# A decode block on one core: ScalarE takes more of the last heads' sums, the second modulation is issued earlier, and the gate's products go to TensorE

## The chip, the cores and the metric

The kernel runs on one core of one Trainium2 chip. The metric is the device time of one execution in microseconds (us); the median of three runs of the kernel before is 1065.96 us (1065.53 to 1066.04). Each core has TensorE (PE, matmuls; PEld is its weight loads), VectorE (DVE), ScalarE (ACT), GpSimd (POOL), the queue of SyncE (SP) that issues the DMAs here, and 16 DMA engines.

## The reference

One token (D = 640) passes through an adaptive-LayerNorm block. The attention reads a cache of 32 heads, 8192 positions, 192 elements, keys and values, all float32:

```
mod = silu(c) @ w_mod                      # six vectors: sa, ca, ga, sb, cb, gb
h = layernorm(x) * (1 + ca) + sa
q = (h @ wq)  per head
p = softmax(q . K^T * 192 ** -0.5);  o = p . V
x = x + ga * (o @ wo)
h = layernorm(x) * (1 + cb) + sb
x = x + gb * (relu(h @ w1 + b1) ** 2 @ w2 + b2)
```

## The kernel before

The caches are 403 MB of the 452 MB that are read, so most of the program is a stream of heads. SyncE's queue issues, head by head, one load of a head's keys (6 MB, with a query or output weight behind them in most heads) and one of its values (6 MB). All of them, and the four weight tiles at the start and the end, share a ring of three slots (`slot`, line 54): each load waits until the tile three places earlier has been read to the end. At the end of the ring the second modulation `wm1_t` (L315 to L321; it also holds the last output weight) takes the slot of head 30's values, `w1_t` (L322; with the gate's weight behind it, L325) that of head 31's keys, and `w2_t` (L328) that of head 31's values. Each is loaded in pieces, and a reader waits for the piece that it needs.

The program order is the order on each engine; nothing is rescheduled. Partition p holds 64 positions of a head. `keys(h)` (L201) multiplies them by the query on VectorE (L213, in place) and then sums the 192 products of each position in three ways: GpSimd folds the upper half of `nf` positions onto the lower (L214) and VectorE reduces the folded 96 (L221); ScalarE sums `na` positions, one ACTIVATE with an accumulator each (L217); VectorE reduces the remaining `a` positions directly (L218). On VectorE the order is L213, L218, whatever `between` puts there (L219: in odd heads the gather of the output weight, three instructions at L154), then L221, which waits for GpSimd. Heads 0 to 29 do this in one part with 28 folded, 4 on ScalarE and 32 direct. Head 30 does it in two halves, head 31 in four quarters, because their keys are loaded in as many pieces (`K_PARTS`):

```
K_PARTS = {H - 2: 2, H - 1: 4}
N_ACT = {H - 2: 8, H - 1: 16}
```

`softmax(h)` (L224) takes the maximum over all partitions through TensorE and writes the exponentials by ScalarE (L236). `own(h-1)` (L257) is VectorE's work on the previous head's output: a masked multiply (L272) and two reductions (L275). `turn` (L278) makes columns of two heads' output by three matmuls (L282) and a ScalarE copy (L284). `values(h)` (L242) is 24 matmuls on TensorE (L249, L253).

After the last head the order is: `own(31)`, `turn`, the attention output `att` (L337, L340), its copy by ScalarE (L343), the second modulation `ps_mod` (20 matmuls, L348), x1 = x + ga * att (L351, L352), its LayerNorm (from L128), the first MLP layer `ps_f` (20 matmuls, L361), relu squared and transposition on VectorE (L364, L365, L106), then on VectorE the gate's products with silu(c) (`weigh`, L147 and L149), and on TensorE the first half of the second layer `ps_y` (24 matmuls, L376), the gate's column sums `ps_g` (4 matmuls, L383), the second half of `ps_y`, and the two last VectorE steps (L391, L392) and the store.

The profile has two records for each float32 matmul, so that 20 matmuls are listed as x40.

Of the kernel before, what the change touches and what calls it, by code (L numbers as in the profile page):

```python
# [45 lines left out]
def block_kernel(ctx: ExitStack, tc: tile.TileContext, first, kx, vx, wm1, w1, w2, out):  # L46
# [56 lines left out]
    def columns(src, n, name, pool=const, **how):  # L103

        t = pool.tile([P, n // 32, 32], F32, name=name, **how)
        nc.vector.transpose(t.rearrange("p b r -> p (b r)"), src)  # L106
        return t
# [37 lines left out]
    def weigh(to, w):  # L145

        nc.vector.tensor_scalar(to, w[:, 0], e[:, 0:1], None, op0=ALU.mult)  # L147
        for b in range(1, KB):
            nc.vector.scalar_tensor_tensor(to, w[:, b], e[:, b:b + 1], to, op0=ALU.mult, op1=ALU.add)  # L149
# [51 lines left out]
    def keys(h, between):  # L201

        q = qb_t[h // 2][:, DH * (h % 2):DH * (h % 2 + 1)]
        sc = work.tile([P, NPOS], F32, tag="sc", name=f"sc{h}")
        t = k_t[h][:, :KV].rearrange("p (i d) -> p i d", d=DH)
        parts = K_PARTS.get(h, 1)
        n = NPOS // parts
        nf, na = N_FOLD // parts, N_ACT.get(h, 4) // parts
        a, b = n - nf - na, n - na
        for c in range(parts):  # L210
            pr = t[:, c * n:(c + 1) * n]
            s = sc[:, c * n:(c + 1) * n]
            nc.vector.tensor_mul(pr, pr, q[:, None, :].to_broadcast([P, n, DH]))  # L213
            nc.gpsimd.tensor_add(pr[:, a:b, :DH // 2], pr[:, a:b, :DH // 2], pr[:, a:b, DH // 2:])  # L214
            for i in range(b, n):
                jk = work.tile([P, DH], F32, tag="jk", name=f"jk{h}_{c}_{i}", bufs=2)
                nc.scalar.activation(jk, pr[:, i], AF.Copy, accum_out=s[:, i:i + 1])  # L217
            nc.vector.tensor_reduce(s[:, :a], pr[:, :a], axis=AX.X, op=ALU.add)  # L218
            if c == 0:  # L219
                between()  # L220
            nc.vector.tensor_reduce(s[:, a:b], pr[:, a:b, :DH // 2], axis=AX.X, op=ALU.add)  # L221
        return sc
# [34 lines left out]
    def own(h):  # L257

        i, a = h // 2, h % 2
        if not a:  # L260
            os_t[i] = work.tile([P, PW], F32, tag="os", name=f"os{i}")
        to = os_t[i][:, DH * a:DH * (a + 1)]
        if a:
            ri_t[i] = work.tile([P, 2], F32, tag="ri", name=f"ri{i}")
            nc.vector.reciprocal(ri_t[i], sum_t.pop(i))
            nc.vector.tensor_scalar(os_t[i][:, :DH], os_t[i][:, :DH], ri_t[i][:, 0:1], None, op0=ALU.mult)
        scale = ri_t.pop(i)[:, 1:2] if a else 1.0
        m = big(f"own{h}", 1024)
        o = o_t.pop(h)
        d = [(0, 512, to[:, :DA]), (512, 1024, to[:, DA:])]  # L270
        for lo, hi in ([(0, 512), (512, 1024)] if h == H - 1 else [(0, 1024)]):
            nc.vector.scalar_tensor_tensor(m[:, lo:hi], o[:, lo:hi], scale, mask[:, lo:hi], op0=ALU.mult, op1=ALU.mult)  # L272
            for x0, x1, r in d:
                if lo <= x0 < hi:
                    nc.vector.tensor_reduce(r, m[:, x0:x1].rearrange("p (j d) -> p d j", d=r.shape[1]),  # L275
                                            axis=AX.X, op=ALU.add)
# [53 lines left out]
        nc.sync.dma_start(w2_t[:, b0 * D:(b0 + n) * D], w2[:, b0 * D:(b0 + n) * D])  # L330
# [11 lines left out]
    att_s = const.tile([P, DG], F32, name="att_s")  # L342
    nc.scalar.copy(att_s, att[:, :DG])  # L343

    ps_mod = psum.tile([P, 512], F32, tag="q", name="ps_mod", bufs=2)
    for b in range(KB):
        for g in range(G):
            nc.tensor.matmul(ps_mod[32 * g:32 * (g + 1), :3 * DG], e[:, b:b + 1].to_broadcast([P, 32]),  # L348
                             wm1_t[:, b, :, DG * g:DG * (g + 1)], start=(b == 0), stop=(b == KB - 1))
    x1 = const.tile([P, DG], F32, name="x1")  # L350
    nc.vector.tensor_mul(x1, ps_mod[:, :DG], att_s)  # L351
    nc.vector.tensor_add(x1, x1, x_t)  # L352
# [18 lines left out]
    py = psum.tile([P, 512], F32, tag="q", name="ps_y", bufs=2)  # L371

    def second(b0, b1):
        for b in range(b0, b1):
            for g in range(G):
                nc.tensor.matmul(py[32 * g:32 * (g + 1), :DG], fT[:, b], w2_t[:, b, DG * g:DG * (g + 1)],  # L376
                                 start=(b == 0), stop=(b == FB - 1))

    n = W2_CUT[0][1]
# [11 lines left out]
    nc.vector.tensor_mul(y, py[:, :DG], gb)  # L391
    nc.vector.tensor_add(y, y, x1)  # L392
# [44 lines left out]
```

## Time and profile before

| | |
|---|---|
| runs before, median of 3 | 1065.96 us |
| profiled execution, its time | 1065.27 us |
| its span, first to last instruction | 1063.5 us |
| read from memory | 451.82 MB, 425 GB/s over the span |
| busy share: DVE, PE, POOL, ACT | 85%, 34%, 18%, 9% |
| DMA queue of SyncE, share of the 16 engines' time | 98.5% |

The span is what the rows of the trace cover; the execution's own time is 1.77 us longer. Times in the rows are microseconds from the start of the span. A row of the timeline gives start, duration, engine, line, operation, the tile written and those read, the count where equal instructions are merged, and in brackets how long the engine was idle before and on whom it waited. A row of the windows gives for one stretch of time each engine's busy time with its count of instructions, then TensorE's granted clock as a share of full speed, the busy share of the DMA engines and GB/s.

### The profile page before, as it was taken

How to read it: one execution, taken by the hardware profiler on the slowest of the kernel's cores; microseconds unless marked ns; L12 is line 12 of the kernel's file. 1: busy time of each engine (PE TensorE's matmuls, PEld its weight loads, DVE VectorE, ACT ScalarE, POOL GpSimd, SP SyncE). 2: the span in 40 equal slices, each digit the busy share in tenths (PEclk: the TensorE clock that was granted, in tenths of full speed). 3: DMA queues.
4: the chain of work that ended last, by engine and by line, in shares of the span. 5: the costliest groups of instructions: out<-in, count | busy, mean ns of one | idle time of the engine just before them, and what ended most of it. 6: DMA issues, size and time to landing. Idle time of an engine off the chain costs nothing.

```text
span 1063.5 us, 5476 instructions
## 1 busy us (share of the span) xinstructions
PE 366.9 (34%) x2088; PEld 133.7 (13%) x2088; DVE 907.2 (85%) x400; ACT 95.2 (9%) x394; POOL 189.9 (18%) x43
## 2 busy tenths in 40 slices
PE   0324333143432314343222434313343431333355
PEld 0101111011110101111010111101111110110122
DVE  6897898998989899898898988899898889989963
ACT  1010001000010101001010100101010010000210
POOL 0220122221022222012222102222211222221210
PEclk9767656666665666666566666656666665666668
DMA  9999999999999999999999999999999999999994
GB/s 400 439 429 419 443 424 440 430 436 442 427 431 434 437 434 431 430 436 428 442 429 436 435 434 430 436 431 437 434 432 434 428 434 438 434 422 416 432 400 201
DMA packets 11410, 452.17 MB, mean 425 GB/s; under 512 B 1268, under 2 KB 1272, under 8 KB 1656
## 3 DMA queue, kind: packets, MB, share of 16 engines
q1 hardware_dynamic: 11384, 451.83, 98.5%
q8 instruction: 16, 0.26, 0.1%
q14 instruction: 10, 0.08, 0.0%
HBM read 451.82 MB, written 0.00 MB: 425 GB/s over the span
## 4 chain that ended last, share of the span: by engine, by line
DVE 40%; DMA 40%; PE 14%; issue 2%; ACT 1%; POOL 1%; POOLq 0%; DVEq 0%; ACTq 0%; SPq 0%
DMA k<-in_kx 39%; DVE k L213 20%; DVE sc L218 9%; PE ps_o L249 8%; DVE sc L221 4%; DVE acc L154 3%; PE ps_o L253 2%; DMA first_t<-in_first 1%; ACT p L236 1%; POOL k L214 1%; PE ps_sum L121 1%; PE ps_mx L228 1%; DVE ma_w L149 1%; PE ps_f L361 1%; PE ps_q L191 1%
## 5 line engine op out<-in xcount | busy, mean ns | idle before, releaser
L213 DVE TENSOR_TENSOR k<-k,qb 128x12288 f32<-128x12288 f32 (+2 forms) x36 | 415.2, 11534 | 94.1 <-DMA k<-in_kx 90.0
L214 POOL TENSOR_TENSOR k<-k 128x2688 f32<-128x2688 f32 (+2 forms) x36 | 188.6, 5240 | 826.9 <-DVE k L213 782.0
L228 PE MATMUL ps_mx<-ident,mp 128*128 128x128 f32 x32 | 15.1, 473 | 589.3 <-DVE mp L226 589.3
L218 DVE TENSOR_REDUCE sc<-k 128x32 f32<-128x6144 f32 (+2 forms) x36 | 207.1, 5753 | 1.2
L249 PE MATMUL ps_o<-v,p 128*32 128x512 f32 x1024 | 183.5, 882 | 2.6 <-ACT p L236 2.6
L217 ACT ACTIVATE jk<-k 128x192 f32<-128x192 f32 x144 | 50.4, 351 | 532.5 <-DVE k L213 508.9
L221 DVE TENSOR_REDUCE sc<-k 128x28 f32<-128x2688 f32 (+2 forms) x36 | 94.9, 2635 | 2.9 <-POOL k L214 2.9
L228 PEld LDWEIGHTS ps_mx<-ident,mp 128*128 128x128 f32 x32 | 5.8, 181 | 613.9 <-DVE mp L226 593.1
L275 DVE TENSOR_REDUCE os<-own 128x128 f32<-128x512 f32 x64 | 63.7, 1036 | 1.1
L253 PE MATMUL ps_o<-v,p 128*32 128x512 f32 x512 | 60.4, 592 | 0.0
L249 PEld LDWEIGHTS ps_o<-v,p 128*32 128x32 f32 x1024 | 40.0, 154 | 116.3 <-issue 112.9
L191 PE MATMUL ps_q<-k,hR 128*128 128x384 f32 x150 | 52.3, 496 | 1.5 <-DMA k<-in_kx 1.5
L236 ACT ACTIVATE p<-sc,nm 128x512 f32<-128x512 f32 x32 | 23.1, 721 | 304.8 <-DVE nm L230 176.8
L282 PE MATMUL ps_oT<-ones,os 128*128 128x1 f32 x96 | 27.6, 356 | 45.5 <-DVE os L275 33.3
L154 DVE SCALAR_TENSOR_TENSOR acc<-k,oT,acc 128x640 f32<-128x640 f32 x45 | 39.7, 882 | 1.1
L191 PEld LDWEIGHTS ps_q<-k,hR 128*128 128x128 f32 x150 | 27.3, 190 | 29.5 <-issue 10.9
L282 PEld LDWEIGHTS ps_oT<-ones,os 128*128 128x128 f32 x96 | 23.5, 304 | 53.5 <-DVE os L275 36.0
L217 ACT ACTIVATION_READ_ACCUMULATOR jk<-k 128x1 f32 x144 | 26.8, 186 | 0.0
L230 DVE TENSOR_REDUCE nm<-ps_mx 128x1 f32<-128x128 f32 x32 | 9.3, 292 | 18.2 <-PE ps_mx L228 18.2
L272 DVE SCALAR_TENSOR_TENSOR own<-ps_o,ri,mask 128x1024 f32<-128x1024 f32 (+1 forms) x17 | 20.7, 1215 | 3.0 <-PE ps_o L253 3.0
L253 PEld LDWEIGHTS ps_o<-v,p 128*32 128x32 f32 x512 | 15.3, 110 | 41.1 <-issue 41.1
L272 DVE SCALAR_TENSOR_TENSOR own<-ps_o,mask 128x1024 f32<-128x1024 f32 x16 | 19.4, 1215 | 0.0
(87 smaller groups left out, 129.9 us busy)
## 6 DMA issues: line engine op xcount, KB each, us to landing
k<-in_kx SPq DMA_DIRECT2D x29, 7104.0 KB, 27.4
v<-in_vx SPq DMA_DIRECT2D x31, 6144.0 KB, 23.1
k<-in_kx SPq DMA_DIRECT2D x1, 6144.0 KB, 25.5
k<-in_kx SPq DMA_DIRECT2D x2, 3072.0 KB, 20.3
k<-in_kx SPq DMA_DIRECT2D x3, 1536.0 KB, 16.4
first_t<-in_first SPq DMA_DIRECT2D x1, 4173.5 KB, 12.8
v<-in_vx SPq DMA_DIRECT2D x1, 4096.0 KB, 19.8
wm_t<-in_wm SPq DMA_DIRECT2D x1, 3840.0 KB, 21.4
```

The source lines that it names most:

```text
L154: nc.vector.scalar_tensor_tensor(to, w[:, j], s[:, j:j + 1], to, op0=ALU.mult, op1=ALU.add)
L191: nc.tensor.matmul(ps[:, :PW], hR[:, b], w[:, b], start=(b == 0), stop=(b == KB - 1))
L213: nc.vector.tensor_mul(pr, pr, q[:, None, :].to_broadcast([P, n, DH]))
L214: nc.gpsimd.tensor_add(pr[:, a:b, :DH // 2], pr[:, a:b, :DH // 2], pr[:, a:b, DH // 2:])
L217: nc.scalar.activation(jk, pr[:, i], AF.Copy, accum_out=s[:, i:i + 1])
L218: nc.vector.tensor_reduce(s[:, :a], pr[:, :a], axis=AX.X, op=ALU.add)
L221: nc.vector.tensor_reduce(s[:, a:b], pr[:, a:b, :DH // 2], axis=AX.X, op=ALU.add)
L249: nc.tensor.matmul(o_t[h][32 * g:32 * (g + 1), :512], p[:, 4 * c:4 * c + 4].rearrange("p e r -> p (e r)"), t[:, 512 * c:512 * (c + 1)], st ...
L253: nc.tensor.matmul(o_t[h][32 * g:32 * (g + 1), 512:], p[:, 8 * c:8 * c + 8, ::2].rearrange("p e r -> p (e r)"), t[:, 512 * (na + c):512 * ...
L272: nc.vector.scalar_tensor_tensor(m[:, lo:hi], o[:, lo:hi], scale, mask[:, lo:hi], op0=ALU.mult, op1=ALU.mult)
L275: nc.vector.tensor_reduce(r, m[:, x0:x1].rearrange("p (j d) -> p d j", d=r.shape[1]), axis=AX.X, op=ALU.add)
L282: nc.tensor.matmul(pt[:, j:j + 1], os_[:, P * j:P * (j + 1)], ones[:, :1], start=True, stop=True)
```

## The change

In the last three heads the parts and their split are given by one table; a pair is (folded, ScalarE), and the rest of a part's positions is direct. Head 29 is computed in two halves now, though its keys are still one load. ScalarE has 16 positions of head 29 (4 before), 20 of head 30 (8) and 26 of head 31 (16). The folded positions are still 28 in heads 29 and 30, and 16 in head 31 (28 before).

After the last head, `ps_mod` is written ahead of `own(31)` and `turn`; the sum of x1 for the LayerNorm is accumulated by the instruction that adds x; `weigh` for the gate is gone, and in its place TensorE does 20 matmuls with silu(c) as the stationary operand right behind `ps_f`, ahead of all of `ps_y`.

```diff
-N_FOLD = 28
-N_ACT = {H - 2: 8, H - 1: 16}
+SUMS = {H - 3: ((14, 10), (14, 6)), H - 2: ((14, 12), (14, 8)), H - 1: ((4, 7), (4, 7), (4, 7), (4, 5))}
...
-    def layernorm(x, copies, scale1, shift, name):
+    def layernorm(x, copies, scale1, shift, name, s=None):
...
-        s = const.tile([P, 1], F32, name=name + "_s")
-        nc.vector.tensor_reduce(s, x, axis=AX.X, op=ALU.add)
+        if s is None:
+            s = const.tile([P, 1], F32, name=name + "_s")
+            nc.vector.tensor_reduce(s, x, axis=AX.X, op=ALU.add)
...
-        parts = K_PARTS.get(h, 1)
-        n = NPOS // parts
-        nf, na = N_FOLD // parts, N_ACT.get(h, 4) // parts
-        a, b = n - nf - na, n - na
-        for c in range(parts):
+        sums = SUMS.get(h, ((28, 4),))
+        n = NPOS // len(sums)
+        for c, (nf, na) in enumerate(sums):
+            a, b = n - nf - na, n - na
...
+    ps_mod = psum.tile([P, 512], F32, tag="q", name="ps_mod", bufs=2)
+    for b in range(KB):
+        for g in range(G):
+            nc.tensor.matmul(ps_mod[32 * g:32 * (g + 1), :3 * DG], e[:, b:b + 1].to_broadcast([P, 32]),
+                             wm1_t[:, b, :, DG * g:DG * (g + 1)], start=(b == 0), stop=(b == KB - 1))
     own(H - 1)
     oT = turn(NPAIR - 1)
...
-    ps_mod = psum.tile([P, 512], F32, tag="q", name="ps_mod", bufs=2)
...
     nc.vector.tensor_mul(x1, ps_mod[:, :DG], att_s)
-    nc.vector.tensor_add(x1, x1, x_t)
+    s1 = const.tile([P, 1], F32, name="s1")
+    nc.vector.scalar_tensor_tensor(x1, x1, 1.0, x_t, op0=ALU.mult, op1=ALU.add, accum_out=s1)
...
-    gb_w = big("gb_w", D)
-    weigh(gb_w, wg_t)
...
-    second(0, n)
     ps_g = psum.tile([P, 512], F32, tag="sm", name="ps_g", bufs=2)
-    for g in range(G):
-        nc.tensor.matmul(ps_g[32 * g:32 * (g + 1), :DG], ones[:, :32], gb_w[:, DG * g:DG * (g + 1)], start=True, stop=True)
+    for b in range(KB):
+        for g in range(G):
+            nc.tensor.matmul(ps_g[32 * g:32 * (g + 1), :DG], e[:, b:b + 1].to_broadcast([P, 32]),
+                             wg_t[:, b, DG * g:DG * (g + 1)], start=(b == 0), stop=(b == KB - 1))
...
-    second(n, FB)
+    for b in range(FB):
+        for g in range(G):
+            nc.tensor.matmul(py[32 * g:32 * (g + 1), :DG], fT[:, b], w2_t[:, b, DG * g:DG * (g + 1)],
+                             start=(b == 0), stop=(b == FB - 1))
```

The line numbers of the changed kernel differ by one or a few from those of before. On VectorE, head 29 reads as follows before; k_2054 are its keys, sc its sums, acc the output weight's accumulator, and 128x32 means 32 positions.

```order
L213 TENSOR_TENSOR k_2054<-k_2054,qb_1872 128x12288
L218 TENSOR_REDUCE sc_2058<-k_2054 128x32
L154 SCALAR_TENSOR_TENSOR acc<-k_2054,oT_2027,acc 128x640 x3
L221 TENSOR_REDUCE sc_2058<-k_2054 128x28
L226 TENSOR_REDUCE mp_2074<-sc_2058 128x1
```

After, on VectorE at the same place:

```order
L212 TENSOR_TENSOR k_2054<-k_2054,qb_1872 128x6144
L217 TENSOR_REDUCE sc_2058<-k_2054 128x8
L154 SCALAR_TENSOR_TENSOR acc<-k_2054,oT_2027,acc 128x640 x3
L220 TENSOR_REDUCE sc_2058<-k_2054 128x14
L212 TENSOR_TENSOR k_2054<-k_2054,qb_1872 128x6144
L217 TENSOR_REDUCE sc_2058<-k_2054 128x12
L220 TENSOR_REDUCE sc_2058<-k_2054 128x14
L225 TENSOR_REDUCE mp_2102<-sc_2058 128x1
```

The multiply is cut in two, 12 direct positions are gone, and the gather stands in the first half only. On TensorE, from the last matmuls of head 31's values on, the program before reads as follows; ps_oT is `turn`, and counts are matmuls.

```order
L253 MATMUL ps_o_2266<-v_2196,p_2254 32x512 x8
L282 MATMUL ps_oT_2311<-ones,os_2258 128x1 x3
L337 MATMUL att<-acc,ones 32x160 x4
L340 MATMUL att<-wm_t,oT_2315 32x160 x12
L348 MATMUL ps_mod<-wm_t,silu 32x480 x20
L121 MATMUL ps_ln_tm<-ln_s,ones 128x1
L121 MATMUL ps_ln_tv<-ln_ss,ones 128x1
L361 MATMUL ps_f<-w_t,hT_2382 32x384 x20
L376 MATMUL ps_y<-w_t,fT 32x160 x24
L383 MATMUL ps_g<-gb_w,ones 32x160 x4
L376 MATMUL ps_y<-w_t,fT 32x160 x24
```

After, on TensorE at the same place:

```order
L252 MATMUL ps_o_2338<-v_2248,p_2326 32x512 x8
L335 MATMUL ps_mod<-wm_t,silu 32x480 x20
L281 MATMUL ps_oT_2404<-ones,os_2330 128x1 x3
L341 MATMUL att<-acc,ones 32x160 x4
L344 MATMUL att<-wm_t,oT_2408 32x160 x12
L120 MATMUL ps_ln_tm<-s_2431,ones 128x1
L120 MATMUL ps_ln_tv<-ln_ss,ones 128x1
L361 MATMUL ps_f<-w_t,hT_2453 32x384 x20
L371 MATMUL ps_g<-w_t,silu 32x160 x20
L383 MATMUL ps_y<-w_t,fT 32x160 x48
```

`ps_mod` has moved from behind `att` to ahead of `turn`, and `ps_g`, 20 matmuls instead of 4, from the middle of `ps_y` to ahead of it. No DMA is added, removed or put in another place on SyncE's queue.

More of the change, by code (lines that the diff above doesn't have):

```diff
@@ L343, in block_kernel @@
     nc.scalar.copy(att_s, att[:, :DG])
-    ps_mod = psum.tile([P, 512], F32, tag="q", name="ps_mod", bufs=2)
-    for b in range(KB):
-        for g in range(G):
-            nc.tensor.matmul(ps_mod[32 * g:32 * (g + 1), :3 * DG], e[:, b:b + 1].to_broadcast([P, 32]),
-                             wm1_t[:, b, :, DG * g:DG * (g + 1)], start=(b == 0), stop=(b == KB - 1))
     x1 = const.tile([P, DG], F32, name="x1")
     nc.vector.tensor_mul(x1, ps_mod[:, :DG], att_s)
-    nc.vector.tensor_add(x1, x1, x_t)
+    s1 = const.tile([P, 1], F32, name="s1")
+    nc.vector.scalar_tensor_tensor(x1, x1, 1.0, x_t, op0=ALU.mult, op1=ALU.add, accum_out=s1)
     cb1 = const.tile([P, DG], F32, name="cb1")
     nc.scalar.activation(cb1, ps_mod[:, 2 * DG:3 * DG], AF.Copy, bias=1.0)
-    hT2 = columns(layernorm(x1, 32, lambda: cb1, lambda: ps_mod[:, DG:2 * DG], "ln2"), DG, "hT2")
+    hT2 = columns(layernorm(x1, 32, lambda: cb1, lambda: ps_mod[:, DG:2 * DG], "ln2", s1), DG, "hT2")
     pf = psum.tile([P, 512], F32, tag="q", name="ps_f", bufs=2)
@@ L366, in block_kernel @@
     fT = columns(f, FG, "fT", work, tag="qb")
-    gb_w = big("gb_w", D)
-    weigh(gb_w, wg_t)
[L371 to L379, printed above, removed]
-    second(0, n)
     ps_g = psum.tile([P, 512], F32, tag="sm", name="ps_g", bufs=2)
-    for g in range(G):
-        nc.tensor.matmul(ps_g[32 * g:32 * (g + 1), :DG], ones[:, :32], gb_w[:, DG * g:DG * (g + 1)], start=True, stop=True)
+    for b in range(KB):
+        for g in range(G):
+            nc.tensor.matmul(ps_g[32 * g:32 * (g + 1), :DG], e[:, b:b + 1].to_broadcast([P, 32]),
+                             wg_t[:, b, DG * g:DG * (g + 1)], start=(b == 0), stop=(b == KB - 1))
     gb = const.tile([P, DG], F32, name="gb")
@@ L388, in block_kernel @@
     nc.vector.tensor_add(x1, x1, gb2)
-    second(n, FB)
+    py = psum.tile([P, 512], F32, tag="q", name="ps_y", bufs=2)
+    for b in range(FB):
+        for g in range(G):
+            nc.tensor.matmul(py[32 * g:32 * (g + 1), :DG], fT[:, b], w2_t[:, b, DG * g:DG * (g + 1)],
+                             start=(b == 0), stop=(b == FB - 1))
     y = const.tile([P, DG], F32, name="y")
```

## The prediction

> **What bounds the kernel now.** I read the page's DMA queues first, then windows of two microseconds over the end.
>
> ```profile
> q1 hardware_dynamic: 11384, 451.83, 98.5%
> ```
>
> ```profile
> 1024.00:1026.00 2.00, 2.00 (x16) 0.44 (x12) 1.69 (x4) 0.00 (x0) 0.00 (x0) 0.56 0.54 230
> 1026.00:1028.00 2.00, 2.00 (x24) 0.54 (x20) 0.00 (x0) 0.00 (x0) 0.00 (x0) 1.00 0.90 263
> 1044.00:1046.00 2.00, 1.61 (x12) 0.68 (x16) 0.29 (x1) 0.00 (x0) 0.00 (x0) 0.50 0.90 380
> 1050.00:1052.00 2.00, 0.40 (x8) 0.00 (x0) 1.47 (x3) 0.00 (x0) 0.00 (x0) 1.00 0.03 13
> ```
>
> The memory stream runs almost without a gap until 1050 us and is over by 1051; 12 us of computing follow it. So two things limit the end: the stream, whose length the change leaves as it is, and the chain of work behind the last keys. The timeline shows that chain through heads 29, 30 and 31:
>
> ```profile
> 937.97 12.96 DVE L213 TENSOR_TENSOR k<-k,qb 128x12288 f32<-128x12288 f32 x1 [4.13 <-DMA k<-in_kx]
> 951.32 0.35 ACT L217 ACTIVATE jk<-k 128x192 f32<-128x192 f32 x1
> 951.67 0.35 ACT L217 ACTIVATE jk<-k 128x192 f32<-128x192 f32 x1
> 957.43 2.72 DVE L154 SCALAR_TENSOR_TENSOR acc<-k,oT,acc 128x640 f32<-128x640 f32 x3
> 960.07 2.95 DVE L221 TENSOR_REDUCE sc<-k 128x28 f32<-128x2688 f32 x1
> ...
> 973.87 2.95 DVE L218 TENSOR_REDUCE sc<-k 128x14 f32<-128x2688 f32 x1
> 974.15 3.03 POOL L214 TENSOR_TENSOR k<-k 128x1344 f32<-128x1344 f32 x1 [17.03 <-DVE k L213]
> 977.21 1.55 DVE L221 TENSOR_REDUCE sc<-k 128x14 f32<-128x1344 f32 x1 [0.39 <-POOL k L214]
> 978.68 6.55 DVE L213 TENSOR_TENSOR k<-k,qb 128x6144 f32<-128x6144 f32 x1
> ...
> 994.64 3.35 DVE L213 TENSOR_TENSOR k<-k,qb 128x3072 f32<-128x3072 f32 x1
> 998.03 1.15 DVE L218 TENSOR_REDUCE sc<-k 128x5 f32<-128x960 f32 x1
> 998.31 1.63 POOL L214 TENSOR_TENSOR k<-k 128x672 f32<-128x672 f32 x1 [9.98 <-DVE k L213]
> 999.97 0.85 DVE L221 TENSOR_REDUCE sc<-k 128x7 f32<-128x672 f32 x1 [0.79 <-POOL k L214]
> ...
> 1017.48 0.85 DVE L221 TENSOR_REDUCE sc<-k 128x7 f32<-128x672 f32 x1 [0.53 <-POOL k L214]
> ```
>
> VectorE waits for keys for the last time at 937.97. After that it waits only for GpSimd's fold, a few tenths each time: from head 29's multiply on, the end is VectorE's, and in heads 30 and 31 partly GpSimd's. Behind head 31 the chain goes over to TensorE:
>
> ```profile
> 1026.80 1.89 PE L253 MATMUL ps_o<-v,p 128*32 128x512 f32 x16
> 1031.29 1.01 DVE L275 TENSOR_REDUCE os<-own 128x64 f32<-128x512 f32 x1
> 1032.36 0.41 PE L282 MATMUL ps_oT<-ones,os 128*128 128x1 f32 x2 [1.32 <-DVE os L275]
> 1033.23 1.83 PE L340 MATMUL att<-wm_t,oT 128*32 128x160 f32 x24
> 1034.83 4.78 PE L348 MATMUL ps_mod<-wm_t,silu 128*32 128x480 f32 x40
> 1035.12 0.29 ACT L343 COPY att_s<-att 128x160 f32<-128x160 f32 x1 [2.16 <-PE att L340]
> 1039.76 0.32 DVE L351 TENSOR_TENSOR x<-ps_mod,att_s 128x160 f32<-128x160 f32 x1 [7.46 <-PE ps_mod L348]
> 1040.12 0.33 DVE L352 TENSOR_TENSOR x<-x,x_t 128x160 f32<-128x160 f32 x1
> 1044.39 6.01 PE L361 MATMUL ps_f<-w_t,hT 128*32 128x384 f32 x40 [1.75 <-issue]
> 1052.33 1.84 PE L376 MATMUL ps_y<-w_t,fT 128*32 128x160 f32 x48 [1.93 <-issue]
> 1052.70 3.65 DVE L149 SCALAR_TENSOR_TENSOR gb_w<-w_t,silu,gb_w 128x640 f32<-128x640 f32 x4
> 1056.91 3.28 PE L376 MATMUL ps_y<-w_t,fT 128*32 128x160 f32 x48
> 1060.26 0.33 DVE L391 TENSOR_TENSOR y<-ps_y,gb 128x160 f32<-128x160 f32 x1 [2.05 <-PE ps_y L376]
> ```
>
> **Head 29.** Before, multiply to last reduction lasts 25.05 us (937.97 to 963.02). After: two half multiplies, 2 x 6.55 = 13.1. The direct reductions cost 0.2 us a position (2.95 for 14, 1.15 for 5), so 8 positions cost 1.75 and 12 cost 2.55. In the first half, direct 1.75 and gather 2.72 hide the fold of 14 (3.03, started up to 0.3 late); then 1.55. In the second half nothing but 2.55 stands beside the fold, so that VectorE waits until 3.1 after the multiply; then 1.55. Sum 13.1 + 1.75 + 2.72 + 1.55 + 3.1 + 1.55 = 23.8: 1.3 us saved, not the 2.4 of the removed positions.
>
> **Head 30.** The folds keep their size, and VectorE already waits for them (0.39 us after 2.95 of direct work). With 6 or 10 direct positions it waits longer and ends at the same time: 0 saved. A fold might run faster beside an idle VectorE; the rows speak against it, since the fold of 7 took 1.63, half of 3.03 and a little, though VectorE idled through its last 0.79. I take 0.
>
> **Head 31.** Before 23.69 us (994.64 to 1018.33). After, the fold has 4 positions; this size is not in the trace. By the line through 3.03 (14) and 1.63 (7) it takes 1.0; it can't take more than 1.63 or, at 0.2 a position, less than 0.8. The folded reduction falls from 0.85 to 0.55 by the same kind of line. Three quarters of 3.35 + 1.2 (direct work 1.15, or the fold with its late start) + 0.55 = 5.1 and a last one with 7 direct positions of 3.35 + 1.55 + 0.55 = 5.45 make 20.75: 2.9 saved (1.1 if the fold stays at 1.63). Together 4.2 us: values end at 1028.7 - 4.2 = 1024.5, own(31) at 1032.3 - 4.2 = 1028.1.
>
> **ScalarE.** It sums a position each 0.35 us. The twelve of head 30's first half are 4.2 us where the next multiply alone lasts 6.55; the seven of a quarter are 2.5 of 5.1; the last five are 1.75 against VectorE's 2.1. Nothing else is queued behind them before the exponentials. Cost 0; without this cover each would be paid in full.
>
> **Second modulation.** On TensorE's queue `turn` and `att` now stand behind it, and it waits for its weight:
>
> ```profile
> L319 SPq DMA_DIRECT2D wm_t<-in_wm x2: 328/382/435, 1002.3 to 1002.6; - x2
> DMA to landing us min/median/max: 21.4/21.4/21.4
> ```
>
> ```profile
> L330 SPq DMA_DIRECT2D w_t<-in_w x4: 328/443/455, 1028.8 to 1030.1; - x4
> DMA to landing us min/median/max: 17.7/20.1/20.9
> ```
>
> The first piece lands at 1002.3 + 21.4 = 1023.7. The landing of the second (1920 KB) isn't shown; at the stream's 425 GB/s it is 4.6 us later, 1028.3. The stream is full there, so an earlier issue doesn't help. A record is 4.78 / 40 = 0.12: 24 of them from 1024.5 end at 1027.4, the other 16 wait for 1028.3 and end at 1030.2. By then own(31) is done, so `turn`'s three steps run together, 1.0 (0.41 for one); `att` 2.3 (1032.77 to 1035.06); the copy att_s, which lay beside ps_mod, is now on the path, 0.29 and two handovers, 0.4. x1 starts at 1033.9 instead of 1039.76: 5.9 earlier. Of the 4.2 from the heads, 2.1 are eaten here by the wait for the weight; that cover also means that the heads may save 2 us less at no loss.
>
> **Accumulated sum.** One VectorE instruction like L352 (0.33) goes, an accumulator read comes: between 0 and 0.33, I take 0.25. So ps_f starts at 1044.39 - 5.9 - 0.25 = 1038.3 and ps_y may start 7.94 later (1044.39 to 1052.33), at 1046.2.
>
> **Gate.** VectorE's 3.65 and what lies around it leave the path. ps_g has 40 records now, 1.84 / 48 = 0.038 each at full clock and 3.28 / 48 = 0.068 at half: 1.5 to 2.7 us, in the 1.9 us in which VectorE makes fT. Cost 0, or 0.8 at half clock. Its copy and two additions hide behind ps_y.
>
> **Second layer.** 96 records at full clock are 3.7: the computing could end at 1049.9. But w2's first piece landed at 1028.8 + 17.7 = 1046.5 and the last at 1030.1 + 20.9 = 1051.0. These loads can move up only by what the stream idles, and it idles because w1 is issued late:
>
> ```profile
> SPq L324 <- DVE acc L154: 22.2, 1, 22.2
> ```
>
> Head 31's gather, 4.2 us earlier, lets w1 be queued before wm1 is through. The two windows from 1024 fall 0.9 and 0.8 us short of 430 GB/s, 1.7 in all. A landing is that of the slowest of 16 engines, and the windows don't tell whether that one had the gap: 0 to 1.7, I take 0.9. Last landing 1050.1; its 8 records and two handovers 0.4; y at 1050.6 instead of 1060.26. What follows is unchanged.
>
> **The sum.** 9.7 us. Of the profiled execution's 1065.27 that leaves 1055.6; this execution is 0.69 below the median of the runs, 1065.96, which leaves 1056.3. With none of the gap recovered 1057.2; with all of it the computing decides, 1055.7.
>
> A rule weighed here: the first 48 records of ps_y ran at full clock, the last 48 at half after a pause, so rows of before would give 96 records 1.84 + 3.28 = 5.1. The Trainium skill (TensorE: Matmul & The Clock Gate, Part 1) says that the clock rises after about 3.4 us of activity and falls after an idle window as long. By it ps_f's 6 us (0.50 in the windows from 1044) have raised the clock when ps_g begins, and, with the pause gone, 3.7 holds; by the rows alone y would come at 1051.3 to 1052.2. I go with 3.7, since the same rows have 1.00 at 1050.
>
> **The rivals.** First, TensorE stays at half clock at the end. ps_g then ends at 1047.1, and ps_y takes 5.1 to 6.6: 1052.2 to 1053.7, a gain of 8.0 to 6.5, 1058.0 to 1059.5. For it: 0.50 in the windows from 1044; against it: 1.00 from 1050. Chance 0.18.
>
> Second, the heads save nothing, because the short folds cost as much as the long and start late, and GpSimd bounds all the parts. Then ps_mod runs from 1028.7 to 1033.5, x1 starts at 1037.2, ps_y at 1049.5, ending at 1053.2 to 1054.6: 1059.0 to 1060.4. For it: VectorE's waits for POOL; against it: the fold falls with its size. Chance 0.11.
>
> Third, more speed: ps_f gets the full clock and the stream gains beyond the two windows. Then the landing alone decides: 1054.8 to 1055.4. Chance 0.07.
>
> Fourth, no change: both first rivals and ps_mod at half clock too (0.2 a record, an estimate from 0.12 and ps_y's ratio of 0.068 to 0.038; 3.2 more): ps_y would end 3 us before the present end at best and level with it at worst, about 1065. Chance 0.04.
>
> Fifth, slower: ScalarE becomes the bound of head 31. At r us a position its 26 take 26 r + 3.4; from r = 0.73 (5.1 / 7) it sets the pace, and at r = 1.2 head 31 ends 13.9 later than forecast, of which ps_mod's wait absorbs 0.95: y 2.6 after 1060.26, 1068.6. For it: a position costs ScalarE 0.35 and VectorE 0.2. Against it: r would have to be 3.4 times the row. Chance 0.03. The Trainium skill (ScalarE: Activation LUTs, Rules for kernel authors) advises VectorE for additions; the rows agree on the price: the 34 moved positions are 11.9 us of ScalarE for 6.8 of VectorE, so that on one path 5.1 would be lost where I count 4.2 gained. They lie beside each other here.
>
> **How the numbers follow.** The forecast has 0.57 with its own range 1055.7 to 1057.3. The range reaches to the second rival's end, 1060.4, and below to 1054.9, nearly the third's. About 0.2% (2.1 us) is what a measurement of this kernel can tell from no change: faster 0.57 + 0.18 + 0.11 + 0.07 = 0.93, same 0.04, slower 0.03.
>
> **What would show it.** Head 30's halves as long as before with longer waits for POOL; head 29 shorter by 1.3 and head 31 by 2.9; ps_mod's second part waiting for its DMA and ending near 1030, behind own(31); no dip of the DMA share near 1025; ps_y waiting for w2's pieces, the last landing near 1050. I am wrong if head 30 is shorter, if ps_y ends well after the last landing, or if ScalarE ends the parts of head 31.

## The result, and the profile after

The changed kernel takes 1055.86 us (median of 4 runs, 1055.24 to 1056.54) where the kernel before takes 1065.74 (4 runs, 1063.99 to 1066.04): a ratio of 0.9911 with a 95% interval of 0.9894 to 0.9928. That is 9.5 us less by the ratio; the two medians lie 9.9 apart. The profiled execution took 1055.74 with a span of 1053.9. Forecast were 1056.3 and a gain of 9.7. The size is right; which terms made it up is another matter, and the rows show it.

The page of the changed kernel has the stream of SyncE's queue at the same work in a shorter span. 98.5% of 1063.5 is 1047.5 us, and 99.4% of 1053.9 is 1047.6:

```profile
q1 hardware_dynamic: 11384, 451.83, 99.4%
```

The windows over the end, with the same columns as before (the clock, the DMA share and GB/s are the last three). The dip to 0.54 in 1024 to 1026 is gone, and the stream thins out from 1048 on:

```profile
1024.00:1026.00 2.00, 2.00 (x26) 0.48 (x18) 0.00 (x0) 0.00 (x0) 0.00 (x0) 1.00 0.97 404
1026.00:1028.00 2.00, 2.00 (x24) 0.60 (x20) 1.72 (x2) 0.00 (x0) 0.00 (x0) 1.00 0.98 401
1048.00:1050.00 2.00, 1.50 (x40) 0.98 (x37) 0.00 (x0) 0.00 (x0) 0.00 (x0) 1.00 0.34 134
```

The timeline of VectorE and GpSimd through heads 29, 30 and 31 of the changed kernel:

```profile
938.70 6.56 DVE L212 TENSOR_TENSOR k<-k,qb 128x6144 f32<-128x6144 f32 x1 [4.08 <-DMA k<-in_kx]
945.29 1.75 DVE L217 TENSOR_REDUCE sc<-k 128x8 f32<-128x1536 f32 x1
945.58 3.03 POOL L213 TENSOR_TENSOR k<-k 128x1344 f32<-128x1344 f32 x1 [19.01 <-DVE k L212]
946.97 4.17 DVE L154 SCALAR_TENSOR_TENSOR acc<-k,oT,acc 128x640 f32<-128x640 f32 x3
...
962.20 1.55 DVE L220 TENSOR_REDUCE sc<-k 128x14 f32<-128x1344 f32 x1 [0.56 <-POOL k L213]
968.04 6.54 DVE L212 TENSOR_TENSOR k<-k,qb 128x6144 f32<-128x6144 f32 x1
...
977.96 1.55 DVE L220 TENSOR_REDUCE sc<-k 128x14 f32<-128x1344 f32 x1 [1.99 <-POOL k L213]
...
989.12 1.55 DVE L220 TENSOR_REDUCE sc<-k 128x14 f32<-128x1344 f32 x1 [0.95 <-POOL k L213]
995.40 3.35 DVE L212 TENSOR_TENSOR k<-k,qb 128x3072 f32<-128x3072 f32 x1
999.07 1.01 POOL L213 TENSOR_TENSOR k<-k 128x384 f32<-128x384 f32 x1 [9.98 <-DVE k L212]
...
1015.29 0.54 DVE L220 TENSOR_REDUCE sc<-k 128x4 f32<-128x384 f32 x1
```

Head 29 lasts from 938.70 to 963.75, 25.05 us, exactly as before: its gather takes 4.17 where it took 2.72. Head 30 saves nothing and only waits longer for GpSimd (1.99 and 0.95). Head 31 lasts 20.43 (995.40 to 1015.83) instead of 23.69. The keys of head 29 came at 938.70 instead of 937.97. So `values` end 3.26 - 0.73 = 2.5 us earlier, at 1026.17 instead of 1028.69, and not 4.2.

The timeline of TensorE and VectorE behind the last head of the changed kernel:

```profile
1024.28 1.89 PE L252 MATMUL ps_o<-v,p 128*32 128x512 f32 x16
1025.99 4.20 PE L335 MATMUL ps_mod<-wm_t,silu 128*32 128x480 f32 x40
1031.20 1.02 PE L344 MATMUL att<-wm_t,oT 128*32 128x160 f32 x24
1032.62 0.33 DVE L350 TENSOR_TENSOR x<-ps_mod,att_s 128x160 f32<-128x160 f32 x1 [2.71 <-ACT att_s L347]
1037.26 4.90 PE L361 MATMUL ps_f<-w_t,hT 128*32 128x384 f32 x40 [1.75 <-issue]
1041.97 1.54 PE L371 MATMUL ps_g<-w_t,silu 128*32 128x160 f32 x40
1043.41 0.58 DVE L105 STREAM_TRANSPOSE fT<-f 128x384 f32<-128x384 f32 x1
1045.41 1.84 PE L383 MATMUL ps_y<-w_t,fT 128*32 128x160 f32 x48 [1.90 <-DMA w_t<-in_w]
1047.88 1.02 PE L383 MATMUL ps_y<-w_t,fT 128*32 128x160 f32 x24 [0.63 <-DMA w_t<-in_w]
1049.41 1.24 PE L383 MATMUL ps_y<-w_t,fT 128*32 128x160 f32 x24 [0.50 <-DMA w_t<-in_w]
1050.71 0.32 DVE L386 TENSOR_TENSOR y<-ps_y,gb 128x160 f32<-128x160 f32 x1 [6.13 <-PE ps_y L383]
```

x1 starts 7.1 us earlier than before (1039.76), fT is ready at 1043.99, and then `ps_y` waits three times for its weight, 3.0 us in all. The issue row of w2 and SyncE's wait ahead of w1:

```profile
L329 SPq DMA_DIRECT2D w_t<-in_w x4: 327/440/445, 1026.2 to 1027.6; - x4
DMA to landing us min/median/max: 19.0/21.8/22.5
```

```profile
SPq L323 <- DVE acc L154: 18.9, 1, 18.9
```

The first piece lands at 1026.2 + 19.0 = 1045.2, and the last at 1027.6 + 22.5 = 1050.1 (the page lists 22.5 for the last piece, of 320 KB); y follows 0.6 behind. In the kernel before it started 9.3 behind the last landing (1051.0). SyncE's wait for the gather, ahead of w1, is 3.3 us shorter than the 22.2 of before, and the dip near 1025 is closed; e1 and e2 below show that the heads' new split closed it. By these rows the end is a landing now; e5 and e6 test it.

### The profile page after: what moved, and what is told of

Its sections match the earlier page's. It is cut to its first block, busy times and chain, and to the rows that moved or that the text cites. A ratio compares the mean times of both kernels' runs of the same rounds, so it can differ in the third digit from the quotient of the medians.

```text
span 1053.9 us, 5606 instructions
## 1 busy us (share of the span) xinstructions
PE 364.5 (35%) x2120; PEld 133.2 (13%) x2120; DVE 898.9 (85%) x398; ACT 107.0 (10%) x462; POOL 187.7 (18%) x44
## 3 DMA queue, kind: packets, MB, share of 16 engines
q1 hardware_dynamic: 11384, 451.83, 99.4%
## 4 chain that ended last, share of the span: by engine, by line
DMA 43%; DVE 41%; PE 13%; ACT 1%; issue 1%; POOL 1%; SPq 0%; DVEq 0%; ACTq 0%; POOLq 0%
DMA k<-in_kx 39%; DVE k L212 21%; DVE sc L217 9%; PE ps_o L248 8%; DVE sc L220 5%; DVE acc L154 4%; PE ps_o L252 3%; DMA w_t<-in_w 2%; DMA first_t<-in_first 1%; ACT p L235 1%; POOL k L213 1%; PE ps_sum L120 1%; PE ps_mx L227 1%; DVE ma_w L149 1%; PE ps_q L191 1%
## 5 line engine op out<-in xcount | busy, mean ns | idle before, releaser
L213 POOL TENSOR_TENSOR k<-k 128x2688 f32<-128x2688 f32 (+2 forms) x37 | 186.4, 5038 | 826.6 <-DVE k L212 782.2
L217 DVE TENSOR_REDUCE sc<-k 128x32 f32<-128x6144 f32 (+6 forms) x37 | 202.9, 5483 | 1.3
L216 ACT ACTIVATE jk<-k 128x192 f32<-128x192 f32 x178 | 62.1, 350 | 527.9 <-DVE k L212 513.2
L216 ACT ACTIVATION_READ_ACCUMULATOR jk<-k 128x1 f32 x178 | 33.2, 186 | 0.0
```

## The experiments

My theory after the result (the stream theory): in the changed kernel the last landing of w2 sets the end, so that the parts of the change do not add up, and what makes the chain of computing shorter or a little longer counts for nothing. The rival (the chain theory): the chain sets the end, and each part undone costs its full price. Times are medians with the ratio to the kernel before, run on the same chip; the last columns are of the profiled execution, the landing being the last issue plus the longest time to landing. One execution of each kernel was profiled, and it need not be the median one: that of e1 was the fastest of twelve, those of e4 and e7 the slowest.

| kernel | us | ratio, 95% | last landing of w2 | y starts | between |
|---|---|---|---|---|---|
| changed kernel | 1055.86 | 0.9911 (0.9894-0.9928) | 1050.1 | 1050.71 | 0.6 |
| e1 heads only | 1063.13 | 0.9975 (0.9965-0.9985) | 1050.0 | 1054.86 | 4.9 |
| e2 tail only | 1057.39 | 0.9924 (0.9911-0.9937) | 1051.8 | 1052.38 | 0.6 |
| e3 modulation behind | 1058.74 | 0.9939 (0.9926-0.9951) | 1050.5 | 1053.72 | 3.2 |
| e4 gate back | 1056.41 | 0.9914 (0.9899-0.9929) | 1052.0 | 1052.55 | 0.6 |
| e5 stream shorter | 1052.91 | 0.9878 (0.9863-0.9893) | 1045.8 | 1047.16 | 1.4 |
| e6 stream longer | 1061.31 | 0.9954 (0.9941-0.9966) | 1053.5 | 1055.31 | 1.8 |
| e7 head 0 earlier | 1054.75 | 0.9894 (0.9880-0.9907) | 1050.2 | 1050.75 | 0.6 |
| e8 heads better | 1053.63 | 0.9884 (0.9870-0.9897) | 1048.1 | 1048.73 | 0.6 |

**e1, the heads alone:** the kernel before with the new table of sums and nothing else.

```diff
...
+SUMS = {H - 3: ((14, 10), (14, 6)), H - 2: ((14, 12), (14, 8)), H - 1: ((4, 7), (4, 7), (4, 7), (4, 5))}
...
```

> The kernel before with the new split of the sums in heads 29 to 31 alone. Stream theory (in the changed kernel the last landing of w2 sets the end, and the computing has 1.4 us to spare at ps_y's start and 2.9 at its end) and chain theory (the landing only comes at the same time; each part shortens the chain by its own price and the prices add up to the whole gain) agree here, because the end of the kernel before lies 9 us behind the last landing: head 31 is 3.3 us shorter, head 29 and head 30 give nothing, and y comes 3.2 us earlier: about 1062.5 us against 1065.7 of before. If head 29's gather weren't slowed, 1.3 more. The last landing should be near 1050 in this kernel already, since w1 is queued before wm1 is through.

The ratio is worth 2.7 us, near the 3.2 expected. It is what the rows of the changed kernel give for the heads (2.5), and not the 4.2 of the prediction. The computing is 4.9 us behind the last landing here, so nothing of the gain is hidden. The 12 runs lie between 1059.87 and 1064.89, far wider than those of the changed kernel. In the profiled one, the fastest, y is 5.4 us earlier than in the profile of before, and not by the heads alone: `ps_mod` took 5.91 (4.78 before), but `ps_f` took 4.71 (6.01 before), and the second half of `ps_y` ran at full clock (timeline of e1):

```profile
1052.98 1.81 PE L374 MATMUL ps_y<-w_t,fT 128*32 128x160 f32 x48
```

It took 3.28 in the kernel before. That the clock makes the scatter of the twelve was not shown. The DMA share has no dip here (1.01 in 1024 to 1026).

**e2, the tail alone:** the changed kernel with the split of the sums that the kernel before has.

```diff
-SUMS = {H - 3: ((14, 10), (14, 6)), H - 2: ((14, 12), (14, 8)), H - 1: ((4, 7), (4, 7), (4, 7), (4, 5))}
+SUMS = {H - 2: ((14, 4),) * 2, H - 1: ((7, 4),) * 4}
```

> The changed kernel with the sums split as before (head 29 in one part, 4 of 32 on ScalarE in head 30's halves, 4 of 16 in head 31's quarters): only the early second modulation, the accumulated sum and the gate on TensorE are left of the change. Chain theory: the heads' 3.3 us come back in full, 1059.1 us. Stream theory: of the 3.3, 2.9 are slack at the end, and w1 is queued late again by about a microsecond, so 0.5 to 1.2 us: 1056.4 to 1057.1.

The median is 0.3 above the stream theory's range and 1.7 below the chain theory's number. The ratio gives 8.1 us without the heads; 2.7 and 8.1 would be 10.8 where both together bring 9.5. Taking the heads away costs 1.4 by the ratios (their intervals overlap), less than the 2.5 that they are worth on the chain. x1 starts at 1035.65, 3.03 later than in the changed kernel, and y only 1.67 later. The heads' remaining worth is on the stream. Without them SyncE waits 21.7 for the gather ahead of w1 and issues it at 1025.53 instead of 1022.96, and the dip of before is back: the two windows are 1.8 us short of 430 GB/s, and the last piece of w2 lands 1.7 later (windows of e2, then its timeline):

```profile
1024.00:1026.00 2.00, 2.00 (x12) 0.39 (x8) 1.76 (x4) 0.00 (x0) 0.00 (x0) 0.50 0.58 246
1026.00:1028.00 2.00, 2.00 (x20) 0.55 (x16) 0.00 (x0) 0.00 (x0) 0.00 (x0) 0.82 0.82 220
```

```profile
1051.07 1.24 PE L383 MATMUL ps_y<-w_t,fT 128*32 128x160 f32 x24 [0.98 <-DMA w_t<-in_w]
```

**e3, the modulation behind `att` again:** the changed kernel with `ps_mod` at its old place.

```diff
-    ps_mod = psum.tile([P, 512], F32, tag="q", name="ps_mod", bufs=2)
...
     att = psum.tile([P, 512], F32, tag="q", name="att", bufs=2)
...
+    ps_mod = psum.tile([P, 512], F32, tag="q", name="ps_mod", bufs=2)
...
```

> The changed kernel with the second modulation back behind att, all else as changed. The chain from own(31) to x1 gets 3.8 us longer: turn can begin at once, att ends near 1031.8, ps_mod near 1036.3 instead of 1030.2. Chain theory: 1059.7 us. Stream theory: ps_y could start 2.5 us after w2's first piece has landed and needs 3.7 us from there, which ends 1.0 us later than now: 1056.9 us.

Neither was right: 1058.74 lies between. The chain got longer than either had priced it, since `ps_mod` took 6.03, not 4.20. x1 starts 6.42 later than in the changed kernel (1039.04), and `ps_y` runs through without a wait (timeline of e3):

```profile
1032.51 6.03 PE L347 MATMUL ps_mod<-wm_t,silu 128*32 128x480 f32 x40
1050.19 3.47 PE L383 MATMUL ps_y<-w_t,fT 128*32 128x160 f32 x96 [0.57 <-ACT gb L374]
```

Of those 6.42 the end shows 3.0 (y at 1053.72 instead of 1050.71). The stretch from x1 to `ps_f` was 0.4 shorter here, and the slack that the chain has in the changed kernel, its 3.0 us of waiting for w2, took the rest. With the price corrected, the chain theory would give the full 6.4, 1062.3, and the stream theory what is left beyond the slack. So the stream theory stands; in this kernel the chain is the later of the two.

**e4, the gate's products on VectorE again,** between the halves of `ps_y`, in the changed kernel.

```diff
-                             wg_t[:, b, DG * g:DG * (g + 1)], start=(b == 0), stop=(b == KB - 1))
...
+    weigh(gb_w, wg_t)
...
+    second(0, n)
...
+    second(n, FB)
```

> The changed kernel with the gate's products back on VectorE behind fT and its column sums between the two halves of ps_y. VectorE's 4.1 us lie between fT (1044.0) and ps_g (1048.2 to 1049.0); the first half of ps_y runs beside them, the second half needs 1.8 to 3.3 us after 1049.0. Chain theory: the gate's price, about 4 us, comes back: 1059.9 us. Stream theory: 0.3 to 1.7 us, 1056.2 to 1057.6 us.

0.3 us by the ratio, which the intervals don't tell from nothing. The 3.65 on VectorE lie beside the first half of `ps_y` and its wait for the weight, and are done at 1050.06, ahead of the last landing at 1052.0 (timeline of e4):

```profile
1046.41 3.65 DVE L149 SCALAR_TENSOR_TENSOR gb_w<-w_t,silu,gb_w 128x640 f32<-128x640 f32 x4
1047.54 1.84 PE L376 MATMUL ps_y<-w_t,fT 128*32 128x160 f32 x48 [3.42 <-DMA w_t<-in_w]
```

The chain theory's 1059.9 falls. From the end of fT (1045.94) the chain with the gate on VectorE needs 4.47 until the second half of `ps_y` begins and 1.84 for that half, 6.3 us, where e5 shows 3.6 for the chain without it: 2.7 more, just inside the 3.0 of slack. With the other parts in place, this part of the change is covered by the stream, though narrowly.

**e5 and e6, the stream 1600 KB shorter or longer.** e5 leaves the gate's weight out; e6 loads it once more, ahead of w2.

In e5:

```diff
-    nc.sync.dma_start(w1_t[:, KB * FF:KB * (FF + D)], w1[:, KB * FF:])
-    wg_t = w1_t[:, KB * FF:KB * (FF + D)].rearrange("p (b n) -> p b n", b=KB)
+    wg_t = w1_t[:, :KB * D].rearrange("p (b n) -> p b n", b=KB)
```

In e6:

```diff
+    nc.sync.dma_start(w1_t[:, KB * (FF + D):KB * (FF + D) + 3200], w1[:, KB * FF:])
```

> The changed kernel without the load of the gate's weight (1600 KB); ps_g reads the first columns of w1 in its place, so that the gate's values aren't the reference's, and all work on the engines is as before. Stream theory: w2's pieces land 3.9 us earlier (1600 KB at 425 GB/s), and then the computing sets the end: fT at 1044.0, 96 records in 3.7, y near 1047.9 instead of 1050.7: 2.8 us less, 1053.1. Chain theory (the computing sets the end already): no change, 1055.9 us.

> The changed kernel with the gate's weight loaded a second time into unused columns, ahead of w2's loads: 1600 KB more in the stream, read by nobody. Stream theory: the last landing and the end come 3.9 us later, 1059.7 us. Chain theory: the computing up to fT doesn't feel it, and of ps_y only the last records wait: at most 1 us, 1056.9.

Both move the end, though neither touches the computing: 3.5 us less and 4.6 more by the ratios, with intervals clear of the changed kernel's (e5's only just). e5 has the whole of `ps_y` in one piece, as soon as its input is there (timeline of e5); the last landing is 4.3 earlier (1045.8), the end 3.5, and what is left over is the chain:

```profile
1043.63 3.47 PE L382 MATMUL ps_y<-w_t,fT 128*32 128x160 f32 x96 [0.57 <-ACT gb L373]
```

In e6 the last landing is 3.4 later and y 4.6. The other 1.2 go with TensorE's clock, which fell while it waited: the 96 records took 6.14, where 3.47 as in e5 would have ended at 1052.6, so that only the last landing, at 1053.5, would have held them (timeline of e6, then its windows):

```profile
1049.10 6.14 PE L384 MATMUL ps_y<-w_t,fT 128*32 128x160 f32 x96 [5.26 <-DMA w_t<-in_w]
```

```profile
1046.00:1048.00 2.00, 0.00 (x0) 0.00 (x0) 0.00 (x0) 0.00 (x0) 0.00 (x0) 0.95 0.95 403
1048.00:1050.00 2.00, 0.90 (x16) 0.80 (x20) 0.00 (x0) 0.00 (x0) 0.00 (x0) 0.50 0.99 416
```

These two runs separate the theories most plainly: the end follows the length of the stream in both directions, until the chain is met.

**e7 and e8, can it go further?** e7 gives head 0, for which the stream's first slots wait, more sums on ScalarE and fewer on VectorE; e8 does that and takes folded positions from heads 29 and 30, so that GpSimd no longer bounds them. The edit is e8's; e7 has its first entry alone.

```diff
-SUMS = {H - 3: ((14, 10), (14, 6)), H - 2: ((14, 12), (14, 8)), H - 1: ((4, 7), (4, 7), (4, 7), (4, 5))}
+SUMS = {0: ((16, 20),), H - 3: ((8, 12), (8, 10)), H - 2: ((8, 12), (8, 10)), H - 1: ((4, 7), (4, 7), (4, 7), (4, 5))}
```

> The changed kernel with head 0's sums split anew (16 folded, 20 on ScalarE, 28 direct instead of 28, 4, 32): its keys are read to the end about 2 us earlier, so that head 1's values are queued 2 us earlier, where the stream runs empty for a moment (head 1's keys have landed at 59.0, the values are issued at 57.2 and land 16.3 later, where a load of this size follows its forerunner by 14.5 elsewhere). Stream theory: what the stream gains there, 0.4 to 1.7 us, comes out at the end in full: 1054.2 to 1055.5 us. Chain theory: head 0 lies 880 us ahead of the chain that ends last, nothing changes: 1055.9 us.

> The kernel of the run with head 0's new split, and heads 29 and 30 split so that neither the gather nor VectorE's last reduction waits for GpSimd: 8 folded in each half, 12 on ScalarE in the first and 10 in the second. Head 29 should take 23.2 us instead of 25.05 and head 30 2.4 us less than now. Chain theory: 4.3 us less than the changed kernel, 1051.6 us. Stream theory: only what the stream gains, as with head 0 alone and a few tenths more because head 30's values are issued earlier: 1053.9 to 1055.4 us.

e7's median, 1054.75, lies in the stream theory's range, but the intervals of e7 and of the changed kernel overlap, so that the time alone doesn't separate the theories. The windows do better. From 1040 on, the DMA share over 20 us is 0.43 in the changed kernel, 0.35 in e7 and 0.32 in e8, so that 8.6, 7.0 and 6.4 us of stream are left there: e7's stream is 1.6 ahead, within the 0.4 to 1.7 that were expected. The profiled run of e7, its slowest, shows nothing of it at the end (y at 1050.75): after its stream had thinned out, a share of 0.06, about one engine of the 16, went on until the last landing at 1050.2 (windows of e7):

```profile
1046.00:1048.00 2.00, 2.00 (x36) 1.70 (x32) 0.00 (x0) 0.00 (x0) 0.00 (x0) 0.50 0.47 188
1048.00:1050.00 2.00, 2.00 (x60) 1.79 (x52) 0.00 (x0) 0.00 (x0) 0.00 (x0) 0.87 0.06 23
```

e8 takes 1053.63 (1053.49 to 1054.01), by the ratio 2.9 less than the changed kernel, with intervals that just overlap. Its head 29 lasts 22.95 and its head 30 20.31 (25.05 and 22.63 in the changed kernel), x1 starts at 1030.25, 2.4 earlier (1.3 of it because head 29's keys came at 937.44), `ps_mod` now waits for its weight, and `ps_y` still waits for w2 (timeline of e8):

```profile
944.32 1.81 POOL L213 TENSOR_TENSOR k<-k 128x768 f32<-128x768 f32 x1 [19.01 <-DVE k L212]
946.50 2.72 DVE L154 SCALAR_TENSOR_TENSOR acc<-k,oT,acc 128x640 f32<-128x640 f32 x3
...
1026.01 1.82 PE L335 MATMUL ps_mod<-wm_t,silu 128*32 128x480 f32 x16 [1.90 <-DMA wm_t<-in_wm]
...
1043.59 1.84 PE L383 MATMUL ps_y<-w_t,fT 128*32 128x160 f32 x48 [2.11 <-DMA w_t<-in_w]
```

4.4 us off the two heads brought some 1.1 beside e7: so far are the medians apart, and the intervals lie over each other. e8 came out 0.3 below the stream theory's range and 2.0 above the chain theory's number. Its last landing is 2.0 earlier than the changed kernel's. Of the 2.2 us that its stream is ahead from 1040 on, e7's head 0 accounts for 1.6; where the other 0.6 come from stays open.

**e9, the gather beside a long fold.** Heads 23, 25 and 27 of the changed kernel get other splits, with the gather behind four direct positions.

```diff
+EARLY = (H - 9, H - 7, H - 5)
+SUMS = {H - 9: ((28, 0),), H - 7: ((1, 10),), H - 5: ((1, 0),), H - 3: ((14, 10), (14, 6)), H - 2: ((14, 12), (14, 8)), H - 1: ((4, 7), (4, 7), (4, 7), (4, 5))}
...
+            if h in EARLY:
+                nc.vector.tensor_reduce(s[:, :4], pr[:, :4], axis=AX.X, op=ALU.add)
                 between()
+                nc.vector.tensor_reduce(s[:, 4:a], pr[:, 4:a], axis=AX.X, op=ALU.add)
...
```

> The gather of head 29 (three steps with two tensor inputs on VectorE, line 154) took 4.17 us in the changed kernel and 2.72 us in the kernel before. Three earlier heads, which wait for their keys and so should leave the end where it is, are given other splits, and in them the gather stands right behind a direct sum of only 4 positions: head 23 with 28 positions folded by GpSimd and none on ScalarE, head 25 with one folded and ten on ScalarE, head 27 with one folded and none on ScalarE; head 29 stays as in the changed kernel. Theory 1, GpSimd's fold holds up VectorE's steps with two tensor inputs: the gather of head 23 ends about 2.7 us after the end of a fold of some 5.9 us, so it takes 7 to 8 us; those of heads 25 and 27 take 2.7 us each; head 29 takes 4.2 us again. Theory 2, ScalarE's sums hold it up: head 23 takes 2.7 us, head 25 about 4.2 us, head 27 2.7 us. If neither, all three take 2.7 us. The time stays that of the changed kernel, 1055.9 us, within 1 us by both.

The timeline of e9 has the gathers of heads 23, 25 and 27, and GpSimd's fold in head 23. Behind it, from a narrower window, stands the first of head 23's three steps by itself:

```profile
764.54 5.85 POOL L214 TENSOR_TENSOR k<-k 128x2688 f32<-128x2688 f32 x1 [25.34 <-DVE k L213]
765.13 7.78 DVE L155 SCALAR_TENSOR_TENSOR acc<-k,oT,acc 128x640 f32<-128x640 f32 x3
...
831.20 2.72 DVE L155 SCALAR_TENSOR_TENSOR acc<-k,oT,acc 128x640 f32<-128x640 f32 x3
...
893.82 2.72 DVE L155 SCALAR_TENSOR_TENSOR acc<-k,oT,acc 128x640 f32<-128x640 f32 x3
```

```profile
765.13 5.94 DVE L155 SCALAR_TENSOR_TENSOR acc<-k,oT,acc 128x640 f32<-128x640 f32 x1
```

The first step took 5.94 where a step of the gather takes 0.9 (2.72 for three): it ended at 771.07, the fold at 770.39, so it stood until the fold was over. The profile shows the step as running all that time, with no wait in brackets. The ten sums on ScalarE (830.3 to 833.8), most of them beside the gather of head 25, cost it nothing, and in e8, where the fold is over before the gather begins, ScalarE's sums cost nothing either: 2.72. Head 29 has 4.17 again in e9. So it was GpSimd's fold that ate the saving of head 29.

The time was a miss for both theories: 1063.06 in its one run (the kernel before took 1066.08 beside it), 7.2 us above the changed kernel where no difference was expected. I had taken a head that waits for its keys to be free of cost. It isn't, because the values are loaded into a slot that the last sum releases. The issue of the next head's values behind head 23 and the DMA share, in the changed kernel and then in e9 (timeline of SyncE's queue, windows):

```profile
776.25 0.33 SPq L100 DMA_DIRECT2D v<-in_vx  x1
```

```profile
770.00:780.00 10.00, 2.15 (x11) 1.08 (x15) 9.22 (x10) 0.81 (x2) 0.29 (x1) 0.50 1.00 433
780.00:790.00 10.00, 10.00 (x54) 3.26 (x46) 8.16 (x2) 0.00 (x0) 0.00 (x0) 0.79 0.98 420
```

```profile
782.26 0.33 SPq L101 DMA_DIRECT2D v<-in_vx  x1
```

```profile
770.00:780.00 10.00, 0.00 (x0) 0.00 (x0) 9.93 (x5) 0.00 (x0) 0.39 (x1) 0.50 0.85 369
780.00:790.00 10.00, 6.17 (x35) 1.97 (x39) 9.37 (x7) 0.81 (x2) 0.00 (x0) 0.54 0.78 302
```

Issued 6.0 later, the load leaves the stream 3.5 us short in these two windows (0.15 and 0.20 of ten). Heads 25 and 27 had more direct work on VectorE as well, and the values behind them are issued 5.2 and 7.3 later. Counted in bytes over windows of 20 us, 760 to 780 moved 403 GB/s instead of 437, 780 to 800 moved 358 instead of 429, and 900 to 920 moved 392 instead of 429: at 433 GB/s 1.6 + 3.3 + 1.7 = 6.6 us. Head 29's multiply starts at 945.40 instead of 938.70: the 6.7 are there before the last heads begin, and they stay to the end. A gap in the stream, 280 us ahead of the end, was not made good.

## Why the prediction was right

The time and the reason for it hold: two things limit the end, the chain of computing behind the last keys and the stream, and the change brings the first down onto the second. The last landing was forecast for 1050.1 and came at 1050.1; y for 1050.6, and came at 1050.71. Since the landing sets the end, errors in the chain did not show in the time, and it had several. That `values` ended 2.5 earlier and not 4.2 is made up of head 29 (1.3 less than forecast), head 31 (0.4 more) and keys that came 0.7 later.

- **Head 29** saved 0, not 1.3. The failed step is "direct 1.75 and gather 2.72 hide the fold of 14": the gather does not run beside the fold, as e9 showed, and came out at 4.17. VectorE's and GpSimd's work were laid side by side as if independent; in the rows of before the gather starts behind the fold (957.43, the fold of 5.87 having begun at 951.25), so that no row had shown the two at once.
- **Head 30** saved 0, as forecast, with longer waits for GpSimd. e8 shows the other half of it: with 8 folded positions a part, it does get shorter.
- **Head 31** saved 3.26 for 2.9. The term mis-sized is a quarter's length: the multiplies start 5.18, 4.94 and 4.92 apart, where 5.1 was taken. The fold of 4, which the trace didn't have, took 1.01 for 1.0.
- **ScalarE** cost 0.35 a position (178 in all) and held up nothing, so that the fifth rival fell. In head 31 it was close: ScalarE's last sum ended at 1015.71, VectorE's last reduction at 1015.83.
- **Second modulation.** `ps_mod` ended at 1030.19, forecast 1030.2, by luck: it began 1.5 later than forecast (1025.99 for 1024.5), its records took 0.6 less (4.20 for 4.78), and the wait of 0.9 for its weight, which was one of the signs I named, is not there. The weight's second piece was priced at 1028.3; in e5 and e6, whose pages list it, it lands 23.8 behind its issue, near 1027, and the changed kernel needs it at 1028.5. The wait is there in e8, where `values` end earlier (1.90 us ahead of the last 16 records), and in e9. The prediction's 2.1 that the wait eats of the heads' 4.2 doesn't follow from its own terms either: 1028.3 less 1027.4 is 0.9. `turn` and `att` took 2.1 us together, not 3.3: the clock was still up behind `ps_mod`. x1 came at 1032.62, 1.3 before the forecast.
- **Accumulated sum.** It saved 0.35, for 0.25: the LayerNorm's first matmul starts 0.74 behind x1 (1032.62 to 1033.36), where it was 1.09 (1039.76 to 1040.85). But from x1 to `ps_f` it is 4.64 us, 4.63 before. The clock took the saving back: the LayerNorm's two small matmuls took 0.54 and 0.56, as the clock fell to 0.50 under the first of them, where they took 0.38 and 0.35 before. In e3 they took 0.38 and 0.35 again, and the stretch is 4.28.
- **First layer and gate.** `ps_f` took 4.90, not 6.0, as the clock rose under it (0.50 in 1038 to 1040, 0.93 in the next two), and `ps_g` 1.54, the lower of the two prices. fT was ready at 1043.99, not 1046.2.
- **Second layer.** The 96 records cost 3.47 in one piece (e5), near the 3.7 taken and not the 5.1 that the rows of before would give. By the Trainium skill (TensorE: Matmul & The Clock Gate, Part 1) the clock should have been up by then, and the runs agree: 1.00 in the window from 1048 of the changed kernel. But it decided next to nothing: from 1045.41, when the first piece had landed, 3.5 us end at 1048.9, ahead of the last landing, and 5.1 at 1050.5, 0.4 behind it.
- **Stream.** 0.9 of the 0 to 1.7 was the middle of a range without a reason for the middle. It fits the row of w2's issue, but e2, e4 and e7 have landings from 1050.2 to 1052.0 with the same bytes: that the landing was hit to the tenth is luck. Behind it, eight records and two handovers took 0.6 and not 0.4; 1050.1 and 0.4 would have been 1050.5, where the prediction wrote 1050.6.

The parts do not add up, as two limits imply and the prediction's sum did not spell out. By the ratios the tail alone is worth 8.1 and the heads alone 2.7; in the changed kernel, undoing the heads costs 1.4, the modulation's place 3.0, the gate's products 0.3.

## What to carry to other kernels

Where a stream of loads and a chain of computing end close together, work out both ends apart; the later one is the time, and past that point a shorter chain is worth only what it lets the stream start earlier. When two engines are said to run side by side, ask whether a row of the trace has ever shown these two instructions at once. In a ring of slots, an engine that waits for its data is not free: what it finishes last releases the next load, and a gap there can be carried to the end, as in e9.

## What the runs showed of the hardware

- The gather's step, a VectorE instruction with two tensor operands, stood still while GpSimd's fold ran: the first step took 5.94 instead of 0.9, and ended 0.7 after the fold (e9). The fold kept its time (5.85, 5.87 before). Reductions, with one operand, didn't suffer: 1.75 for 8 positions beside a fold (changed kernel) and 9.95 for 49 without one (e9) lie on one line of 0.2 a position. The Trainium skill (SBUF — State Buffer, Who interferes with whom) has this: a VectorE instruction with two SBUF inputs contends with a GpSimd instruction that reads SBUF. These runs agree.
- The same 40 records of `ps_mod` took 4.20 right behind `values` (changed kernel, clock 1.00), and behind `att`, after pauses of TensorE, 4.78 (before), 5.91 (e1) and 6.03 (e3). So the place in the order moves the clock that a matmul gets, and at one and the same place it still differs from run to run.
- A wait for a load can cost more than its length. In e6 TensorE idled 5.26 ahead of `ps_y`, the granted clock fell to 0.50 by the window in which it resumed, and 1.2 us came on top; in the changed kernel the wait of 1.90 left the clock at 1.00. The length of the pause alone doesn't decide: behind `att` of the changed kernel, whose last matmul ended at 1032.2, the clock was 0.95 in 1033.0 to 1033.5 and 0.50 from there.
- The last landing can trail the stream as a whole. In e7 a DMA share of 0.06 (0.06 x 16 = 1.0, an estimate of one engine) was still at work in 1048 to 1050, and the last landing came at 1050.2 as in the changed kernel, though the stream as a whole was 1.6 us ahead.
